# Six blocks of 500, 500, 500, 512, 500 and 500 spectrum columns for two batches, in place of 502 each

## The chip, the core and the metric

The kernel runs on one core of one Trainium2 chip. The core has a matrix engine (PE, with a separate row for its weight loads, PEld), a vector engine (DVE), a scalar engine (ACT), a general engine (POOL) and a queue engine (SP) that issues the DMAs. The metric is the device time of one execution in microseconds (us), lower is better.

## What is computed

```python
X = np.fft.fft(x, axis=1)              # x: 8 batches, 3008 positions, 256 features
X = np.fft.fft(X, axis=2)
x = X.real.astype(np.float32).reshape(8 * 3008, 256)
h = x @ w_in                           # 256 -> 2048
r = np.maximum(h, 0.0)
g = s * (r * r) + b
return g @ w_out                       # 2048 -> 256
```

The real part of the transform of real data has symmetries, so only 1506 spectrum columns of each batch are formed, and each gives two of the 3008 rows of the result.

## The kernel before

**Stages.** For each batch the kernel loads eight tiles of x (`load`), transforms them with matrix tables (`transform`, one call for each half `ph` of the columns), and splits the result into a high and a low part, `spec_h` and `spec_l` (`store`, ACT for the high and POOL for the low part). The 1506 columns are cut into three blocks of `NT = 502`. Each block goes through 16 steps of an MLP, one for each 128 of the 2048 hidden features: 8 batches, 3 blocks and 16 steps make 384 steps.

**One step.** `first_layer` runs six matmuls of 502 columns on PE (two kinds, and three products for each: high by high, high weights by low data, low weights by high data) into PSUM. DVE adds a rank-one term from `ebc`, the broadcast Nyquist row of this block, and forms two rows of hidden values in `h` (L830 to L832). ACT squares them and rounds them to the high part `gh` (L845 to L847), POOL or DVE forms the low part `gl` (L851). `second_layer` runs twelve matmuls of 502 columns (L868): two rows `pm`, two output halves `dh`, and three products. So a step has 18 streams through PE, each behind a weight load of its own of 128 by 128. In the steps of the very first block the streams of row `pm = 0` are 504 columns wide: two more columns of ones give sums of the weights.

**Memory.** A tile that PE streams is `[P, 2, HALF]` with `HALF = 512`: two rows of 2048 bytes in each partition. The 502 columns, of 4 bytes each, start at a row's first byte and end at byte 2008; 504 columns end at byte 2016. They are of the type fp32r, which goes through PE once. The feature fold of the weights and the transforms (L370, L656) run on plain fp32.

**Order.** What each engine does in which order is written out by hand, as a string of letters for the first batch (`START`) and one for each later batch (`BATCH`). `_in_order` fixes the order of each engine's instructions, so nothing is reordered while the kernel runs. The transform of batch n+1 lies among the steps of batch n. `finish` adds scale and bias after a block's last step (L887) and writes it out with two DMAs on SP (L891); `load_e` fetches the next block's `ebc` on SP (L962).

Of the kernel before, what the change touches and what calls it, by code (L numbers as in the profile page):

```python
# [9 lines left out]
F32 = mybir.dt.float32  # L10
# [25 lines left out]
SPLIT = 754  # L36

# [62 lines left out]
def _columns():  # L100

    ks, turned = [], []
    for ph in range(2):
        m = _quarters(ph)
        n = H if ph else Q
        both = np.stack([m, n - m], axis=1)
        sg = np.stack([_SIGMA, -_SIGMA])[None, :, :, None] + 0 * both
        k = both * (1 if ph else 2)
        k, sg = k.reshape(4, 8, G), sg.reshape(4, 8, G)
        if ph == 0:  # L110
            parts = [
                (0, lambda v: v.reshape(2, 4 * G)[:, :-1]), (1, lambda v: v.reshape(4, 2 * G)[:, :-1]),
                (2, lambda v: v), (3, lambda v: v[:, :-1]),
            ]
        else:
            parts = [(0, lambda v: v), (3, lambda v: v), (1, lambda v: v[:, :-1]), (2, lambda v: v[:, :-1])]
# [108 lines left out]


def _in_order(tc):
# [42 lines left out]
def kernel(ctx: ExitStack, tc: tile.TileContext, xq, xn, dft, turn, feat, w_in, w_out, s, b, out):  # L270
# [176 lines left out]
    def nyquist(ph, t, room):  # L447
# [62 lines left out]
                stop=i == len(work) - 1,  # L510
            )
        yield
        e = room if ph else outp.tile([P, 2 * NT], F32, name="e", tag="o")
        to = 0
        for r in range(4):
            at, groups, size, kept = PLACES[ph][r]
# [14 lines left out]

    def block_of(su, blk):
        if (su, blk) not in spec_tiles:
            spec_tiles[su, blk] = [spec_part(part) for part in "hl"]
# [86 lines left out]
    def store(su, ph, parts, low_engine=nc.gpsimd):  # L621

        pieces = []
        for r, o in parts:
            at, groups, size, kept = PLACES[ph][r]
            n = groups * kept
            first = at // NT
            if (at + n - 1) // NT == first:
                pieces.append((
                    first, at - first * NT, n, lambda v, g=groups: v.rearrange("p k (a g) -> p k a g", a=g),  # L630
                    o.rearrange("p k (a g) -> p k a g", a=groups)[:, :, :, :kept],
                ))
            else:
                cut = (first + 1) * NT - at
                pieces.append((first, NT - cut, cut, lambda v: v, o[:, :, :cut]))
                pieces.append((first + 1, 0, n - cut, lambda v: v, o[:, :, cut:]))
# [182 lines left out]

    def first_layer(su, blk, j, ebc):  # L820
        mh, ml = block_of(su, blk)
        held, ps = two_banks()
        ps = ps[:, :, :NT]
        fj = slice(j * P, (j + 1) * P)
        for kind in range(2):
            for i, (w, m) in enumerate(((wd_h, mh), (wd_h, ml), (wd_l, mh))):
                nc.tensor.matmul(ps[:, kind], w[:, kind, fj], m[:, kind], start=i == 0, stop=i == 2)  # L827
        yield
        h = act.tile([P, 2, NT], F32, name="h")
# [4 lines left out]
        step = (su * NBLK + blk) * NJ + j  # L834
        rows = (slice(1, 2), slice(0, 1)) if step in HALVED else (slice(0, 2),)
        gh, gl = halves_of("gh"), halves_of("gl")
        if (su, blk) == (0, 0):

            nc.gpsimd.memset(gh[:, 0, NT:NT + 2].bitcast(F32), 1.0)
            nc.gpsimd.memset(gl[:, 0, NT:NT + 2].bitcast(F32), 0.0)  # L840
        for pm in rows:
            if step in SQUARES_OF_STEPS_ON_VECTOR:
                nc.vector.scalar_tensor_tensor(h[:, pm], h[:, pm], 0.0, h[:, pm], op0=ALU.max, op1=ALU.mult)
            else:
                nc.scalar.activation(h[:, pm], h[:, pm], AF.Relu)  # L845
                nc.scalar.activation(h[:, pm], h[:, pm], AF.Square)  # L846
            nc.scalar.copy(gh[:, pm, :NT], h[:, pm])  # L847
        yield gh, gl
        engine = nc.vector if step in LOWS_OF_STEPS_ON_VECTOR else nc.gpsimd
        for pm in rows:  # L850
            engine.tensor_sub(gl[:, pm, :NT], h[:, pm], gh[:, pm, :NT].bitcast(F32))  # L851
        yield

    def second_layer(po, j, g, sums, end, order):
        gh, gl = g
        start, stop = j == 0, j == NJ - 1
        for pm in order:
            n = NT + 2 if sums and pm == 0 else NT
            work = [
                (dh, l, r, first, last)  # L860
                for l, r, first, last in ((wo_h, gh, True, False), (wo_l, gh, False, False), (wo_h, gl, False, True))
# [9 lines left out]
                )  # L871

    def finish(su, blk, po):
        if (su, blk) == (0, 0):
            for dh in range(2):
                nc.vector.tensor_scalar(bias[:, dh:dh + 1], po[dh][:, NT:NT + 1], sb_b, None, ALU.mult)
        last = (su, blk) == (NB - 1, NBLK - 1)
        for pm in range(2):
            o = outp.tile([P, 2, NT], F32, name="o")
            for dh in range(2):  # L880
                args = sb_s, bias[:, dh:dh + 1]

                dst, src = o[:, dh], po[2 * pm + dh][:, :NT]
# [17 lines left out]
    lo = [spec_part("l") for _ in range(2)]  # L901
    room = read.tile([P, 1024], F32, name="room", tag="spec_h")
    hi = [spec_part("h") for _ in range(2)]
# [49 lines left out]
    step = 0  # L953

    def load_e(n):
        su, blk = divmod(n, NBLK)
        ebc[n] = small.tile([P, NT], F32, name="ebc")
        for ph in range(2):
            first, last = max(0, blk * NT - SPLIT * ph), min((blk + 1) * NT - SPLIT * ph, e_dram[ph].shape[1])
            if first < last:  # L960
                at = first + SPLIT * ph - blk * NT
                nc.sync.dma_start(ebc[n][:, at:at + last - first], e_dram[ph][su, first:last].partition_broadcast(P))  # L962

    def first():
        nonlocal step
        su, blk, j = step // (NBLK * NJ), step // NJ % NBLK, step % NJ
        step += 1
        n = su * NBLK + blk
        if j == NJ // 2 + (NJ // 4 if n == 0 else 0) and n + 1 < NB * NBLK:
# [9 lines left out]
    def second():  # L979
        nonlocal po  # L980
        (su, blk, j), g = pending.pop(0)
        if j == 0:
            po = [ps_o.tile([P, 512], F32, name="po") for _ in range(4)]
        second_layer(
            po, j, g, (su, blk) == (0, 0), (su, blk, j) == (NB - 1, NBLK - 1, NJ - 1),
            (1, 0) if (su * NBLK + blk) * NJ + j in HALVED else (0, 1),
        )
        if j == NJ - 1:
            finish(su, blk, po)
# [24 lines left out]
            next(work[what])  # L1014

    su = 1
    while step < NB * NBLK * NJ:
        work = {}
        if su < NB - 1:
            work = {"l": load(su + 1), "v": transform(su + 1, 0), "o": transform(su + 1, 1)}  # L1020
        for what in BATCH.split():
            if what == "L" and step < NB * NBLK * NJ:
                first()
                go_on_first()
                next(lows.pop(0))
# [40 lines left out]
```

## Time and profile before

| | |
|---|---|
| time, median of 3 runs | 1664.88 us (1663.75 to 1666.82) |
| the profiled execution's own time | 1666.82 us |
| its span | 1663.8 us |
| busy: PE, DVE, ACT, POOL | 1647.9, 1291.8, 1241.5, 908.7 us |
| HBM traffic | 40 GB/s over the span |

The span is what the profiler sees from the first to the last instruction; 3.0 us of the execution lie around it. Busy time is a sum over the whole span. PE's rows are pipelined, so a PE that is busy all the time need not be at its peak: its pace is read from where its matmuls start.

### The profile page before, as it was taken

The page shows a single profiled execution, that of the slowest core. Times are in us where ns is not written, and L with a number is a line of the kernel's source. Part 1 is how long each engine was busy: PE and PEld are TensorE (multiplying, and loading weights), DVE is VectorE, ACT ScalarE, POOL GpSimd, SP SyncE. Part 2 cuts the span into 40 slices and gives each one's busy share as a digit, 9 for nine tenths or more (in the row PEclk, how much of TensorE's full clock was granted, in tenths as well). Part 3 has the DMA queues.
Part 4 walks back from the last instruction along what each step waited for, and adds up shares of the span by engine and source line. Part 5 has one row for each costly group of instructions (what it writes and reads, how often), then busy time and mean ns, then how long its engine had stood idle before and what let it go on. Part 6 is the DMA issues. An engine that isn't in the chain of part 4 may idle for free.

```text
span 1663.8 us, 21402 instructions
## 1 busy us (share of the span) xinstructions
PE 1647.9 (99%) x7592; PEld 1375.8 (83%) x7592; DVE 1291.8 (78%) x2010; ACT 1241.5 (75%) x1300; POOL 908.7 (55%) x538
## 2 busy tenths in 40 slices
PE   9999999999999999999999999999999999999998
PEld 5788888888888888888888888888888888888887
DVE  7999989997779767798677976889767887776453
ACT  4986666677687777877777777777778777687776
POOL 5663334555565555655656556555555555565554
PEclk9999999999999999999999999999999999999999
DMA  8211201120012100120000200112101110000000
GB/s 235 77 39 51 69 20 32 39 70 31 1 32 73 36 32 1 41 73 26 32 28 22 80 10 31 32 33 67 39 3 32 39 50 32 1 32 28 4 26 25
DMA packets 25680, 67.44 MB, mean 41 GB/s; under 512 B 4931, under 2 KB 10371, under 8 KB 25574
## 3 DMA queue, kind: packets, MB, share of 16 engines
q1 hardware_dynamic: 25574, 66.09, 12.8%
q8 instruction: 59, 0.97, 0.2%
q14 instruction: 47, 0.39, 0.1%
HBM read 41.35 MB, written 24.73 MB: 40 GB/s over the span
## 4 chain that ended last, share of the span: by engine, by line
PE 92%; DVE 4%; DMA 2%; issue 1%; ACT 0%; POOLq 0%; SPq 0%; DVEq 0%
PE po L868 59%; PE ab L827 30%; PE ab L656 3%; DVE h L830 1%; DVE h L831 1%; DMA raw<-in_w_in 1%; DMA xt<-in_xq 1%; DVE h L832 1%; PE ab L370 0%; DVE cs L566 0%; DVE xt L561 0%; DMA dft_sb<-in_dft 0%; DMA room<-in_xn 0%; DVE xt L563 0%; DVE uv L403 0%
## 5 line engine op out<-in xcount | busy, mean ns | idle before, releaser
L851 POOL TENSOR_TENSOR gl<-h,gh 128x1004 fp32r<-128x1004 f32 (+1 forms) x365 | 801.7, 2197 | 689.8 <-ACT gh L847 485.0
L845 ACT ACTIVATE h<-h 128x1004 f32<-128x1004 f32 (+1 forms) x380 | 395.4, 1041 | 340.9 <-DVE h L832 339.7
L830 DVE SCALAR_TENSOR_TENSOR h<-ebc,wny,ab 128x502 f32<-128x502 f32 x384 | 281.7, 734 | 299.9 <-PE ab L827 294.6
L868 PE MATMUL po<-gh,wo_h 128*128 128x502 f32 (+1 forms) x1536 | 471.9, 388 | 0.0
L868 PE MATMUL po<-gl,wo_h 128*128 128x502 f32 (+1 forms) x1536 | 468.2, 386 | 0.2 <-POOL gl L851 0.2
L868 PE MATMUL po<-gh,wo_l 128*128 128x502 f32 (+1 forms) x1536 | 468.4, 386 | 0.0
L847 ACT CAST gh<-h 128x1004 fp32r<-128x1004 f32 (+1 forms) x385 | 397.6, 1033 | 34.3 <-PE po L868 15.6
L846 ACT ACTIVATE h<-h 128x1004 f32<-128x1004 f32 (+1 forms) x380 | 396.1, 1042 | 12.1
L868 PEld LDWEIGHTS po<-gl,wo_h 128*128 128x128 f32 x1536 | 288.3, 188 | 55.8 <-POOL gl L851 0.7
L868 PEld LDWEIGHTS po<-gh,wo_l 128*128 128x128 f32 x1536 | 288.4, 188 | 55.3
L868 PEld LDWEIGHTS po<-gh,wo_h 128*128 128x128 f32 x1536 | 285.2, 188 | 51.9
L827 PE MATMUL ab<-spec_h,wd_h 128*128 128x502 f32 x768 | 299.5, 390 | 7.8 <-DVE h L832 6.9
L827 PE MATMUL ab<-spec_l,wd_h 128*128 128x502 f32 x768 | 296.2, 386 | 0.2 <-DVE spec_l L642 0.2
L827 PE MATMUL ab<-spec_h,wd_l 128*128 128x502 f32 x768 | 296.1, 386 | 0.0
L832 DVE TENSOR_TENSOR h<-h,ab 128x502 f32<-128x502 f32 x384 | 260.4, 678 | 13.3
L831 DVE TENSOR_TENSOR h<-h,ab 128x502 f32<-128x502 f32 x384 | 260.2, 678 | 13.2
L827 PEld LDWEIGHTS ab<-spec_h,wd_h 128*128 128x128 f32 x768 | 144.2, 188 | 40.0 <-DVE h L832 11.3
L827 PEld LDWEIGHTS ab<-spec_h,wd_l 128*128 128x128 f32 x768 | 144.1, 188 | 27.7
L827 PEld LDWEIGHTS ab<-spec_l,wd_h 128*128 128x128 f32 x768 | 144.2, 188 | 26.8 <-DVE spec_l L642 0.5
L887 DVE TENSOR_SCALAR o<-po,sb_s,bias 128x502 f32<-128x502 f32 x94 | 68.8, 793 | 8.5 <-PE po L868 8.4
L642 POOL TENSOR_TENSOR spec_l<-o,spec_h 128x384 fp32r<-128x384 f32 (+4 forms) x75 | 60.3, 828 | 18.6 <-ACT spec_h L639 18.1
L561 DVE TENSOR_TENSOR xt<-xt 96x512 f32<-96x512 f32 x56 | 65.1, 1163 | 0.0
(125 smaller groups left out, 735.0 us busy)
## 6 DMA issues: line engine op xcount, KB each, us to landing
xt<-in_xq SPq DMA_DIRECT2D x64, 384.0 KB
out<-o SPq DMA_DIRECT2D x46, 502.0 KB
raw<-in_w_in SPq DMA_DIRECT2D x8, 512.0 KB
raw<-in_w_out SPq DMA_DIRECT2D x8, 512.0 KB
ebc<-e_dram SPq DMA_DIRECT2D x16, 251.0 KB
ebc<-e_dram SPq DMA_DIRECT2D x8, 126.0 KB
out<-o SPq DMA_DIRECT2D x4, 251.0 KB
ebc<-e_dram SPq DMA_DIRECT2D x8, 125.0 KB
```

What stands on the lines that cost most here:

```text
L561: add(t[:, 0::2], t[:, 0::2], t[:, 1::2])
L642: low_engine.tensor_sub(lo, src, hi.bitcast(F32))
L827: nc.tensor.matmul(ps[:, kind], w[:, kind, fj], m[:, kind], start=i == 0, stop=i == 2)
L830: nc.vector.scalar_tensor_tensor(h[:, 0], ebc, wny[:, j:j + 1], ps[:, 0], op0=ALU.mult, op1=ALU.add)
L831: sub(h[:, 1], h[:, 0], ps[:, 1])
L832: add(h[:, 0], h[:, 0], ps[:, 1])
L845: nc.scalar.activation(h[:, pm], h[:, pm], AF.Relu)
L846: nc.scalar.activation(h[:, pm], h[:, pm], AF.Square)
L847: nc.scalar.copy(gh[:, pm, :NT], h[:, pm])
L851: engine.tensor_sub(gl[:, pm, :NT], h[:, pm], gh[:, pm, :NT].bitcast(F32))
L868: nc.tensor.matmul(po[2 * pm + dh][:, :n], l[:, j, dh * P:(dh + 1) * P], r[:, pm, :n], start=start and first, stop=stop and last,)
L887: nc.vector.tensor_scalar(dst, src, *args, ALU.mult, ALU.add)
```

## The change

Two consecutive batches share six blocks. The even batch gives three blocks of 500 columns and keeps its last 6 in a small tile `rest`; the odd batch's first block is those 6 behind 506 of its own, 512 in all, and two blocks of 500 follow. The six blocks have 3012 columns together, as before. Tiles that hold 512 columns start at a row's first byte; those of 500 start four elements, 16 bytes, further on and end at byte 2016. The places of the parts in the second half of the columns are reordered. Output and `ebc` of the shared block come from two batches, so some DMAs become two.

```diff
-NT = 502
-NBLK = 3
+NT = NK
+NBLK = 1
+SHORT = 500
+NBLOCKS = 3
+REST = NK - NBLOCKS * SHORT
...
-    ((754, 1, 192, 192), (1138, 8, 24, 23), (1322, 8, 24, 23), (946, 1, 192, 192)),
+    ((938, 1, 192, 192), (754, 8, 24, 23), (1130, 8, 24, 23), (1314, 1, 192, 192)),
...
+def _stretches(su):
+
+    cuts = (0, SHORT, 2 * SHORT, 3 * SHORT) if su % 2 == 0 else (0, SHORT + REST, 2 * SHORT + REST, NK)
+    own = [(blk, cuts[blk], cuts[blk + 1]) for blk in range(NBLOCKS)]
+    return own + ([(None, cuts[-1], NK)] if su % 2 == 0 else [])
+
+
+def _sources(su, blk):
+
+    _, first, last = _stretches(su)[blk]
+    own = [(su, first, last, 0)]
+    return own + ([(su - 1, NK - REST, NK, last)] if su % 2 and blk == 0 else [])
+
+
+def _width(su, blk):
+    return sum(last - first for _, first, last, _ in _sources(su, blk))
...
-    def halves_of(name):
-
-        return read.tile([P, 2, HALF], F32R, name=name)
-
-    def spec_part(part):
-        return halves_of(f"spec_{part}")[:, :, :NT]
-
+    def halves_of(name, width):
+
+        first = 0 if width == HALF else 4
+        return read.tile([P, 2, HALF], F32R, name=name)[:, :, first:]
+
+    def spec_part(part, width):
+        return halves_of(f"spec_{part}", width)[:, :, :width]
+
+    rest = late.tile([P, 2, REST], F32, name="rest")
...
+                elif blk is None:
+                    nc.scalar.copy(rest, o[:, :, a - at:z - at])
+                else:
+                    pieces.append((blk, a - first, z - a, lambda v: v, o[:, :, a - at:z - at]))
+                if su % 2 and z == SHORT + REST:
+                    pieces.append((blk, z, REST, lambda v: v, rest))
...
-        ps = ps[:, :, :NT]
+        width = _width(su, blk)
+        ps = ps[:, :, :width]
...
-                if last:
-                    nc.sync.dma_start(out[su, blk, :, 2 * pm + dh], o[:, dh])
-            if not last:
-                nc.sync.dma_start(out[su, blk, :, 2 * pm:2 * pm + 2], o)
+                if not last and dh == 0:
+                    continue
+                which = slice(dh, dh + 1) if last else slice(0, 2)
+                for of, a, z, at in _sources(su, blk):
+                    nc.sync.dma_start(
+                        out[of, 0, :, 2 * pm + which.start:2 * pm + which.stop, a:z], o[:, which, at:at + z - a]
+                    )
```

On PE, where the third block of batch 0 gives way to the first of batch 1 (`ab` and `po` are PSUM tiles, `wd` and `wo` the weights of the two layers), the rows before are these:

```order
L868 MATMUL po<-gh,wo_l 128x502 x2
L868 MATMUL po<-gl,wo_h 128x502 x2
L827 MATMUL ab<-spec_h,wd_h 128x502
L827 MATMUL ab<-spec_l,wd_h 128x502
L827 MATMUL ab<-spec_h,wd_l 128x502
```

At the same place of the changed kernel:

```order
L897 MATMUL po<-gh,wo_l 128x500 x2
L897 MATMUL po<-gl,wo_h 128x500 x2
L856 MATMUL ab<-spec_h,wd_h 128x512
L856 MATMUL ab<-spec_l,wd_h 128x512
L856 MATMUL ab<-spec_h,wd_l 128x512
```

No matmul has moved, and PE has as many rows as before; only the widths differ, here 500 and then 512 where 502 stood. The 504 of the first block become 502.

On SP, during the first blocks of batch 1 (`xt` are tiles of x for a later batch, the two `e_dram` tensors hold the two halves of the Nyquist row), the rows before are these:

```order
L962 DMA ebc<-e_dram_109 128x502
L552 DMA xt<-in_xq 96x1024 x2
L891 DMA out<-o 128x1004 x2
L962 DMA ebc<-e_dram_109 128x252
L962 DMA ebc<-e_dram_110 128x250
L552 DMA xt<-in_xq 96x1024 x5
L891 DMA out<-o 128x1004 x2
```

And in the changed kernel:

```order
L995 DMA ebc<-e_dram_109 128x506
L995 DMA ebc<-e_dram_110 128x6
L575 DMA xt<-in_xq 96x1024 x2
L922 DMA out<-o 128x2x500 x2
L995 DMA ebc<-e_dram_109 128x248
L995 DMA ebc<-e_dram_110 128x252
L575 DMA xt<-in_xq 96x1024 x5
L922 DMA out<-o 128x2x506
L922 DMA out<-o 128x2x6
L922 DMA out<-o 128x2x506
L922 DMA out<-o 128x2x6
```

The order is the same; an issue for 6 columns stands behind each one that serves the shared block.

## Rows read from the trace of the kernel before

**Rows 1.** The page: busy time and share of each engine; the chain that ended last.

```profile
PE 1647.9 (99%) x7592; PEld 1375.8 (83%) x7592; DVE 1291.8 (78%) x2010; ACT 1241.5 (75%) x1300; POOL 908.7 (55%) x538
...
PE 92%; DVE 4%; DMA 2%; issue 1%; ACT 0%; POOLq 0%; SPq 0%; DVEq 0%
PE po L868 59%; PE ab L827 30%; PE ab L656 3%; DVE h L830 1%; DVE h L831 1%; DMA raw<-in_w_in 1%; DMA xt<-in_xq 1%; DVE h L832 1%; PE ab L370 0%; DVE cs L566 0%; DVE xt L561 0%; DMA dft_sb<-in_dft 0%; DMA room<-in_xn 0%; DVE xt L563 0%; DVE uv L403 0%
```

**Rows 2.** Windows of one batch each: length, engines' busy us, PE clock, DMA.

```profile
486.00:686.00 200.00, 200.00 (x928) 169.03 (x927) 155.00 (x244) 151.59 (x154) 113.25 (x58) 1.00 0.11 36
686.00:886.00 200.00, 200.00 (x928) 169.02 (x927) 155.28 (x245) 151.57 (x155) 113.19 (x58) 1.00 0.11 36
886.00:1086.00 200.00, 200.00 (x928) 169.02 (x927) 155.53 (x244) 151.55 (x155) 113.26 (x58) 1.00 0.11 36
1286.00:1486.00 200.00, 200.00 (x928) 169.07 (x927) 155.58 (x244) 151.55 (x155) 112.93 (x59) 1.00 0.10 32
```

**Rows 3.** Waits of PE's weight loads, 486 to 1486 us: total, times, longest.

```profile
PEld ab L827 <- DVE h L832: 0.4, 1, 0.4
```

**Rows 4.** The chain from 1560 us: start, duration, engine, count of instructions.

```profile
1560.16 5.36 PE po L868 x24
1565.52 2.68 PE ab L827 x12
```

**Rows 5.** Groups by form: the matmuls that carry the MLP (count | busy, mean ns).

```profile
L868 PE MATMUL po<-gh,wo_h 128*128 128x502 f32 x1504 | 461.9, 388 | 0.0
L827 PE MATMUL ab<-spec_h,wd_h 128*128 128x502 f32 x768 | 299.5, 390 | 7.8 <-DVE h L832 6.9 <-DVE wd_l L297 0.8
L868 PE MATMUL po<-gh,wo_h 128*128 128x504 f32 x32 | 10.0, 393 | 0.0
```

**Rows 6.** Timeline of PE, a step of the first block: start, duration.

```profile
114.22 0.62 PE L868 MATMUL po<-gh,wo_h 128*128 128x504 f32 x2
114.67 0.62 PE L868 MATMUL po<-gh,wo_l 128*128 128x504 f32 x2
115.13 0.61 PE L868 MATMUL po<-gl,wo_h 128*128 128x504 f32 x2
115.58 0.62 PE L868 MATMUL po<-gh,wo_h 128*128 128x502 f32 x2
```

**Rows 7.** Timeline of PE: plain fp32 matmuls of 512 columns, and the next.

```profile
90.43 1.45 PE L370 MATMUL ab<-cs,feat_sb 128*128 128x512 f32 x3
91.72 1.03 PE L656 MATMUL ab<-dft_sb,lf 96*128 96x96 f32 x8
```

**Rows 8.** Timeline of PE: twelve L868 matmuls of one step (502 columns), and the next.

```profile
250.79 0.63 PE L868 MATMUL po<-gh,wo_h 128*128 128x502 f32 x2
...
253.59 1.03 PE L656 MATMUL ab<-dft_sb,cs 96*128 96x96 f32 x8
```

**Rows 9.** Groups by form: the smallest pieces of a block's high and low part.

```profile
L642 POOL TENSOR_TENSOR spec_l<-o,spec_h 128x116 fp32r<-128x116 f32 x8 | 4.0, 498 | 0.0
...
L639 ACT CAST spec_h<-o 128x116 fp32r<-128x116 f32 x8 | 2.3, 284 | 0.0
```

**Rows 10.** Timeline of SP, block ends of one batch: DMA issues.

```profile
800.54 1.78 SPq L891 DMA_DIRECT2D out<-o  x2
802.37 0.44 SPq L962 DMA_DIRECT2D ebc<-e_dram  x1
868.55 1.75 SPq L891 DMA_DIRECT2D out<-o  x2
870.40 1.14 SPq L962 DMA_DIRECT2D ebc<-e_dram  x2
```

More of the change, by code (lines that the diff above doesn't have):

```diff
@@ L115, in _columns @@
         else:
-            parts = [(0, lambda v: v), (3, lambda v: v), (1, lambda v: v[:, :-1]), (2, lambda v: v[:, :-1])]
+            parts = [(1, lambda v: v[:, :-1]), (0, lambda v: v), (2, lambda v: v[:, :-1]), (3, lambda v: v)]
         for r, cut in parts:
@@ L512, in nyquist @@
         yield
-        e = room if ph else outp.tile([P, 2 * NT], F32, name="e", tag="o")
+        e = room if ph else outp.tile([P, 2 * HALF], F32, name="e", tag="o")
         to = 0
@@ L533, in block_of @@
         if (su, blk) not in spec_tiles:
-            spec_tiles[su, blk] = [spec_part(part) for part in "hl"]
+            spec_tiles[su, blk] = [spec_part(part, _width(su, blk)) for part in "hl"]
         return spec_tiles[su, blk]
-    def halves_of(name):
-        return read.tile([P, 2, HALF], F32R, name=name)
-    def spec_part(part):
-        return halves_of(f"spec_{part}")[:, :, :NT]
+    def halves_of(name, width):
[4 more added lines that the diff above has]
+    rest = late.tile([P, 2, REST], F32, name="rest")
     folded = {}
@@ L626, in store @@
             n = groups * kept
[L627 to L636, printed above, removed]
+            for blk, first, last in _stretches(su):
+                a, z = max(at, first), min(at + n, last)
+                if a >= z:
+                    continue
+                if z - a == n:
+                    pieces.append((
+                        blk, at - first, n, lambda v, g=groups: v.rearrange("p k (a g) -> p k a g", a=g),
+                        o.rearrange("p k (a g) -> p k a g", a=groups)[:, :, :, :kept],
+                    ))
+                elif blk is None:
[4 more added lines that the diff above has]
+                    pieces.append((blk, z, REST, lambda v: v, rest))
         views = [[f(t[:, :, at:at + n]) for t in block_of(su, blk)] for blk, at, n, f, _ in pieces]
@@ L828, in first_layer @@
         yield
-        h = act.tile([P, 2, NT], F32, name="h")
+        h = act.tile([P, 2, width], F32, name="h")
         nc.vector.scalar_tensor_tensor(h[:, 0], ebc, wny[:, j:j + 1], ps[:, 0], op0=ALU.mult, op1=ALU.add)
@@ L833, in first_layer @@
         banks.give(held)
-        step = (su * NBLK + blk) * NJ + j
+        step = (su * NBLOCKS + blk) * NJ + j
         rows = (slice(1, 2), slice(0, 1)) if step in HALVED else (slice(0, 2),)
-        gh, gl = halves_of("gh"), halves_of("gl")
+        gh, gl = halves_of("gh", width), halves_of("gl", width)
         if (su, blk) == (0, 0):
-            nc.gpsimd.memset(gh[:, 0, NT:NT + 2].bitcast(F32), 1.0)
-            nc.gpsimd.memset(gl[:, 0, NT:NT + 2].bitcast(F32), 0.0)
+            nc.gpsimd.memset(gh[:, 0, width:width + 2].bitcast(F32), 1.0)
+            nc.gpsimd.memset(gl[:, 0, width:width + 2].bitcast(F32), 0.0)
         for pm in rows:
@@ L846, in first_layer @@
                 nc.scalar.activation(h[:, pm], h[:, pm], AF.Square)
-            nc.scalar.copy(gh[:, pm, :NT], h[:, pm])
+            nc.scalar.copy(gh[:, pm, :width], h[:, pm])
         yield gh, gl
@@ L850, in first_layer, with second_layer @@
         for pm in rows:
-            engine.tensor_sub(gl[:, pm, :NT], h[:, pm], gh[:, pm, :NT].bitcast(F32))
+            engine.tensor_sub(gl[:, pm, :width], h[:, pm], gh[:, pm, :width].bitcast(F32))
         yield
-    def second_layer(po, j, g, sums, end, order):
+    def second_layer(po, j, g, width, sums, end, order):
         gh, gl = g
@@ L857, in second_layer @@
         for pm in order:
-            n = NT + 2 if sums and pm == 0 else NT
+            n = width + 2 if sums and pm == 0 else width
             work = [
@@ L873, in finish @@
     def finish(su, blk, po):
+        width = _width(su, blk)
         if (su, blk) == (0, 0):
             for dh in range(2):
-                nc.vector.tensor_scalar(bias[:, dh:dh + 1], po[dh][:, NT:NT + 1], sb_b, None, ALU.mult)
-        last = (su, blk) == (NB - 1, NBLK - 1)
+                nc.vector.tensor_scalar(bias[:, dh:dh + 1], po[dh][:, width:width + 1], sb_b, None, ALU.mult)
+        last = (su, blk) == (NB - 1, NBLOCKS - 1)
         for pm in range(2):
-            o = outp.tile([P, 2, NT], F32, name="o")
+            o = outp.tile([P, 2, width], F32, name="o")
             for dh in range(2):
                 args = sb_s, bias[:, dh:dh + 1]
-                dst, src = o[:, dh], po[2 * pm + dh][:, :NT]
+                dst, src = o[:, dh], po[2 * pm + dh][:, :width]
                 if last and dh:
@@ L887, in finish @@
                     nc.vector.tensor_scalar(dst, src, *args, ALU.mult, ALU.add)
-                if last:
-                    nc.sync.dma_start(out[su, blk, :, 2 * pm + dh], o[:, dh])
-            if not last:
-                nc.sync.dma_start(out[su, blk, :, 2 * pm:2 * pm + 2], o)
+                if not last and dh == 0:
+                    continue
+                which = slice(dh, dh + 1) if last else slice(0, 2)
[3 more added lines that the diff above has]
+                    )
     tiles = {}
@@ L900 @@
     minus = unit[:R, 2 * R:6 * R].rearrange("p (i l) -> p i l", i=4)
-    lo = [spec_part("l") for _ in range(2)]
+    lo = [spec_part("l", SHORT) for _ in range(2)]
     room = read.tile([P, 1024], F32, name="room", tag="spec_h")
-    hi = [spec_part("h") for _ in range(2)]
+    hi = [spec_part("h", SHORT) for _ in range(2)]
     for k in range(2):
@@ L955, in load_e @@
     def load_e(n):
[L956 to L962, printed above, removed]
+        su, blk = divmod(n, NBLOCKS)
+        ebc[n] = small.tile([P, _width(su, blk)], F32, name="ebc")
+        for of, a, z, at in _sources(su, blk):
+            for ph, (first, last) in enumerate(((0, SPLIT), (SPLIT, NK))):
+                lo, hi = max(a, first), min(z, last)
+                if lo < hi:
+                    nc.sync.dma_start(
+                        ebc[n][:, at + lo - a:at + hi - a],
+                        e_dram[ph][of, lo - first:hi - first].partition_broadcast(P),
+                    )
     def first():
         nonlocal step
-        su, blk, j = step // (NBLK * NJ), step // NJ % NBLK, step % NJ
+        su, blk, j = step // (NBLOCKS * NJ), step // NJ % NBLOCKS, step % NJ
         step += 1
-        n = su * NBLK + blk
-        if j == NJ // 2 + (NJ // 4 if n == 0 else 0) and n + 1 < NB * NBLK:
+        n = su * NBLOCKS + blk
+        if j == NJ // 2 + (NJ // 4 if n == 0 else 0) and n + 1 < NB * NBLOCKS:
             load_e(n + 1)
@@ L984, in second @@
         second_layer(
-            po, j, g, (su, blk) == (0, 0), (su, blk, j) == (NB - 1, NBLK - 1, NJ - 1),
-            (1, 0) if (su * NBLK + blk) * NJ + j in HALVED else (0, 1),
+            po, j, g, _width(su, blk), (su, blk) == (0, 0), (su, blk, j) == (NB - 1, NBLOCKS - 1, NJ - 1),
+            (1, 0) if (su * NBLOCKS + blk) * NJ + j in HALVED else (0, 1),
         )
@@ L1016 @@
     su = 1
-    while step < NB * NBLK * NJ:
+    while step < NB * NBLOCKS * NJ:
         work = {}
@@ L1021 @@
         for what in BATCH.split():
-            if what == "L" and step < NB * NBLK * NJ:
+            if what == "L" and step < NB * NBLOCKS * NJ:
                 first()
```

## The prediction

> **What bounds the kernel now.** I read the page first. PE is busy for 99% of the span, and the chain that ended last runs through PE for 92% of it, nearly all in the two MLP lines [rows 1]. That alone does not say that PE could not go faster, so I went on to the windows, one batch each: from 486 us on PE is busy for 200.00 of 200 us, DVE for some 155, ACT for 152, POOL for 113, and the granted clock is 1.00, the level of 2.4 GHz [rows 2]. The waits say whether PE hangs on somebody: over five batches its weight loads waited once, for 0.4 us [rows 3]. So in the steady part nothing holds PE but PE. The time is the number of matmuls times the distance from one start to the next, and that distance is what the change can move.
>
> **The pace of a stream.** The chain gives starts: 24 matmuls of 502 columns take 5.36 us and 12 take 2.68 us [rows 4], 223.3 ns each. At 2.4 GHz a column is 0.417 ns, so 502 columns are 209.2 ns, and each matmul carries 14.2 ns in which no column goes through. The mean durations of 388 or 390 ns [rows 5] overlap each other and are no pace. Two other widths stand in the trace. Six streams of 504 columns run from 114.22 to 115.58 us [rows 6], 226.7 ns each: two columns more, worth 0.8 ns of clock, cost 3.4 ns. Plain fp32 matmuls of 512 columns run three in 1.29 us [rows 7], 430 ns each, which is twice 215.0: those data go through twice, at half the bytes for each cycle, and carry only 1.7 ns over the clock for each pass of 213.3. And the same 502 columns, with the same instructions, once ran twelve in 2.80 us [rows 8], 233.3 ns each. So a stream's extra time isn't a constant: it depends on the width by more than the clock explains, and can settle at more than one level.
>
> **What the change moves.** A step has 18 matmuls and there are 384 steps: 6912 streams, 1543.5 us at 223.3 ns, 93% of the span. The counts agree (1504 and 32 for one of three products of the second layer, 768 for one of the first) [rows 5]. After the change 5/6 of them, 5760, have 500 columns and start 16 bytes further on, and 1152 have 512 columns from a row's first byte. The columns in total stay the same, 3012 for each pair of batches, so at a fixed extra for each matmul nothing would change.
>
> *A stream of 500 from byte 16.* No row shows this start. From below: the lowest extra that any long stream shows is that of the plain fp32 rows, so 215.0 less 12 columns of 0.417, 210.0 ns. From above: 226.7 ns, what 504 columns take that end at the same byte 2016; the worst level that a row shows is 233.3 less 0.8. I take what the two fp32r widths give when the line through them is carried two columns down: 223.3 - 3.4 = 219.9 ns. They are the nearest rows, of the same type and at the same rate; for the start I put nothing. That is 5760 x 3.4 ns = 19.6 us less.
>
> *A stream of 512.* From below 215.0 ns, the plain fp32 rows for one pass; from above 226.7 + 8 x 0.417 = 230.0, the 504 with its extra kept. The line through 502 and 504 would give 240.3 ns, but it can't hold for long, since it would ask for an extra of 27 ns, more than even the slow level's 24.1. The fp32 rows have the width and the filled row of 2048 bytes, the 504 rows have the type and the rate; I take the middle, 222.5. That is 1152 x 0.8 = 0.9 us less.
>
> *The rest.* ACT gets 8 instructions more, the copies into `rest` and out of it, of 12 elements; POOL 4. The nearest rows, of 116 elements, take 284 ns on ACT and 498 on POOL [rows 9], from above; below lies nothing. That is at most 2.3 and 2.0 us in all, on engines that are idle for 48 and 87 us in each batch [rows 2]. Without that cover they would be worth as much on the path. The larger block makes a step's instructions on DVE, ACT and POOL 2% longer, the shorter ones 0.4% shorter; over a pair of batches that is nothing. SP issues 16 DMAs more. An issue of `out` takes 0.89 us and of `ebc` 0.44 to 0.57 [rows 10], so at most 14 us over the whole run, on a queue that stands still between blocks; behind it wait only tiles of x for a later batch and the next block's `ebc`, due half a block later. I put all of this at 0.
>
> *Whether the others keep up.* A batch now takes 200 us. DVE, the fullest, needs 155.6 [rows 2]; 20 us less over eight batches asks for 197.5, and the whole extra removed for some 189. DVE would then be at 82%. With one wait of 0.4 us in five batches [rows 3] I see no queue that is near its limit, so PE's gain would come through whole.
>
> **The sum.** 19.6 + 0.9 = 20.5 us less. The profiled execution took 1666.82 us, so 1646.3 by its own account; it is the slowest of the three, 1.9 us above the median of 1664.88. Taken to the median: **1644.4 us**, 1.2% faster.
>
> **The rivals.**
>
> *The extra of the 500s goes for the most part.* If it comes from how a row's end meets the next row's start, a width of whole 16-byte pieces and a later start may remove it. For this speak the plain fp32 rows, which show that PE can chain long matmuls with 1.7 ns between them [rows 7], and that the extra reacts so sharply to two columns [rows 4, 6]. Against it: 504 is also a whole number of 16-byte pieces, and it is worse than 502. At the lower bounds: 5760 x 13.3 + 1152 x 8.3 = 76.6 + 9.6 = 86.2 us less, 1578.7 us; with 500 at half way, 216.7, and 512 as now, 38 us less, 1626.9 us.
>
> *Nothing changes.* If each matmul carries a fixed extra and a column only its clock, five streams of 222.5 and one of 227.5 are six of 223.3, and the time stays at 1664.9. For it speaks that the columns are the same in number; against it the 504 rows, which broke that rule by 2.6 ns [rows 6]. The Trainium skill has this rule (TensorE: Matmul & The Clock Gate, Back-to-back issue gap): in a warm stream a matmul follows the last one after its columns at 2.4 GHz and a constant of 2.5 ns. By it 502 columns would take 211.7 ns, and the trace disagrees with that by 11.6 ns; the plain fp32 rows agree with it, pass by pass, within 1 ns. As the page has a constant that doesn't depend on width or start, by the page this change is worth nothing.
>
> *The end counts, and it gets slower.* A stream of 500 from byte 16 ends at byte 2016, just as the 504 do. If the extra hangs on where a row ends, or if the later start is paid as four empty columns, the 500s take what the 504s take: 226.7 ns, 5760 x 3.4 = 19.6 us more, and the 512, at 230.0, 1152 x 6.7 = 7.7 us more: 1692.2 us. It decides from the point at which a 500 costs more than 223.5 ns, with the 512s at their middle. That one width ran at 233.3 as well [rows 8] shows that a worse level is within reach.
>
> **How the numbers follow.** My forecast (500 at about 220 ns, 1632 to 1661 us) has a chance of 0.38, the larger removal (below 1632 us) 0.30, no change within 0.2% 0.11, slower 0.21. 0.2% is about what a measurement of this kernel can tell from no change. So faster 0.68, same 0.11, slower 0.21. For 8 in 10 the range reaches down to 1598 us, which leaves out the deepest third of the second case, 0.1, and up to 1690, which leaves out a good third of the slower one, 0.08.
>
> **What would show it.** In the profile after, the distance between starts decides everything: 24 streams of 500 should take 5.28 us in the chain where 502 took 5.36, and 12 streams of 512 some 2.67. If the 500s stand at 5.05 to 5.2 us, the second case is right; at 5.34 with the 512s at 2.73, the third; at 5.44, the fourth. A window of one batch should still show PE busy throughout, and DVE, ACT and POOL with the same busy time as now; new waits of PE for DVE or POOL in the list of waits would say that the others did not keep up. What would make the forecast wrong is above all the start at byte 16, which no row of the trace has, and a pace that settles at another level.

## The result and the profile after

| | before | after |
|---|---|---|
| time, median | 1665.43 us (4 runs, 1663.75 to 1666.82) | 1678.74 us (4 runs, 1678.45 to 1679.25) |
| span of the profiled execution | 1663.8 us | 1677.3 us |

The ratio is 1.0081 with a 95% interval of 1.0063 to 1.0098: the change makes the kernel 13.3 us slower. The prediction was 1644.4 us, a gain. Among the experiments below one execution, of the kernel before with cheap rows, was a slow one of 5497.44 us; it stands in that version's median of 1660.15 us, which is 1659.83 us without it.

The page of the changed kernel first, busy time and then the chain that ended last, where [rows 1] show the kernel before:

```profile
PE 1645.9 (98%) x7592; PEld 1374.0 (82%) x7592; DVE 1334.0 (80%) x2010; ACT 1242.9 (74%) x1308; POOL 975.6 (58%) x542
...
PE 79%; DVE 14%; issue 3%; DMA 2%; ACT 1%; POOL 0%; POOLq 0%; SPq 0%; DVEq 0%; ACTq 0%
```

PE is busy for 2 us less, but POOL for 67 us more and DVE for 42 us more, with 4 instructions more on POOL and none on DVE. DVE's share of the chain has gone from 4% to 14%. The windows of about one batch, to be held against [rows 2]:

```profile
489.00:691.00 202.00, 199.29 (x928) 168.31 (x926) 163.17 (x244) 151.55 (x157) 121.64 (x59) 1.00 0.12 35
691.00:894.00 203.00, 200.57 (x931) 168.87 (x930) 164.36 (x245) 152.10 (x155) 121.91 (x58) 1.00 0.12 35
```

PE is no longer busy throughout: it stands idle for more than 2 us in each window. DVE has grown by 8 us a batch and POOL by 8; ACT and the clock are as they were. The chain shows the pace of PE's streams, first of 500 columns (600 us on) and then of 512 (1103 us on), as in [rows 4] for 502:

```profile
601.44 2.64 PE po L897 x12
604.08 1.32 PE ab L856 x6
605.40 2.64 PE po L897 x12
...
1107.63 2.72 PE ab L856 x12
1110.35 5.44 PE po L897 x24
```

Twelve streams of 500 take 2.64 us, 220.0 ns each; 24 of 512 take 5.44 us, 226.7 ns each. So the 500s run here at the pace that was forecast, to 0.1 ns, and most of the loss lies elsewhere. I put together all distances between neighbouring starts of MLP matmuls. Those under 240 ns average 223.5 ns before (6729 of them, all of 502 columns), and after 220.6 for the 500s (5531) and 227.9 for the 512s (1126); over all 500s and 512s that is 5663 x 2.9 - 1152 x 4.4 = 11 us gained. The longer distances are pauses. What they hold beyond the median distance of their width was 16.6 us in total before and is 41.0 us after: 24.4 us lost. The two make 13 us, and the span is 13.5 us longer.

The list of waits says who caused the pauses (total us, times, longest). PE, its weight loads, and DVE:

```profile
PE ab L856 <- DVE h L861: 21.0, 22, 1.8
...
PEld ab L856 <- DVE h L861: 34.9, 39, 2.3
...
DVE h L859 <- POOL gl L880: 96.8, 51, 3.9
```

The same three in the kernel before:

```profile
PE ab L827 <- DVE h L832: 6.9, 7, 1.4
...
PEld ab L827 <- DVE h L832: 11.3, 12, 1.8
...
DVE h L830 <- POOL gl L851: 2.2, 2, 1.9
```

So PE waits for DVE, and DVE's first instruction of a step waits for POOL more often than before. Whether these two waits belong together is taken up with the four buffers below. The groups name the work that grew: POOL's low part, and two DVE groups (count | busy, mean ns | idle before and its cause):

```profile
L880 POOL TENSOR_TENSOR gl<-h,gh 128x1000 fp32r<-128x1000 f32 x302 | 715.6, 2370 | 536.8 <-ACT gh L876 442.2 <-DVE h L860 16.5 <-PE ab L856 15.3
L880 POOL TENSOR_TENSOR gl<-h,gh 128x1024 fp32r<-128x1024 f32 x61 | 149.5, 2451 | 98.8 <-ACT gh L876 70.9 <-DVE h L860 16.0 <-PE po L897 5.6
...
L584 DVE TENSOR_TENSOR xt<-xt 96x512 f32<-96x512 f32 x56 | 73.7, 1315 | 0.0
L588 DVE TENSOR_TENSOR cs<-xt 96x256 f32<-96x256 f32 x56 | 61.7, 1101 | 0.7
```

And the same groups before:

```profile
L851 POOL TENSOR_TENSOR gl<-h,gh 128x1004 fp32r<-128x1004 f32 x363 | 799.2, 2202 | 688.5 <-ACT gh L847 483.7 <-DVE h L831 141.1 <-DVE h L830 27.3
L561 DVE TENSOR_TENSOR xt<-xt 96x512 f32<-96x512 f32 x56 | 65.1, 1163 | 0.0
L565 DVE TENSOR_TENSOR cs<-xt 96x256 f32<-96x256 f32 x56 | 39.2, 700 | 0.7
```

POOL's low part has four elements fewer in each partition and takes 168 ns longer, 8%; with 2% more elements it takes 249 ns longer. The two DVE groups belong to the transform and are untouched by the change, yet they take 152 and 401 ns longer. One stretch of the changed kernel's timeline shows how the two hang together (start, duration, idle time before and its cause):

```profile
916.00 2.36 POOL L880 TENSOR_TENSOR gl<-h,gh 128x1000 fp32r<-128x1000 f32 x1 [0.70 <-ACT gh L876]
916.10 2.80 DVE L584 TENSOR_TENSOR xt<-xt 96x512 f32<-96x512 f32 x1
...
919.59 2.34 POOL L880 TENSOR_TENSOR gl<-h,gh 128x1000 fp32r<-128x1000 f32 x1 [1.23 <-ACT gh L876]
...
919.73 2.48 DVE L588 TENSOR_TENSOR cs<-xt 96x256 f32<-96x256 f32 x1
...
922.14 0.41 DVE L589 TENSOR_TENSOR cs<-xt 96x256 f32<-96x256 f32 x1
...
922.48 0.72 DVE L859 SCALAR_TENSOR_TENSOR h<-ebc,wny,ab 128x500 f32<-128x500 f32 x1
...
924.53 0.68 DVE L584 TENSOR_TENSOR xt<-xt 96x512 f32<-96x512 f32 x1
924.66 0.19 PEld L856 LDWEIGHTS ab<-spec_h,wd_h 128*128 128x128 f32 x1 [0.59 <-DVE h L861]
```

An `xt` of 512 elements takes 0.68 us when POOL is quiet (the row at 924.53). The one at 916.10 begins 0.1 us after a low part on POOL, and ends 0.54 us after it, 2.80 us in all. The `cs` at 919.73 does the same, 2.48 us where the next one of the same form, at 922.14, takes 0.41. DVE stands still behind POOL. Then L859 comes late, with it the release of PSUM after L861, and the weight load of PE's next first layer waits 0.59 us. The step's own instructions on DVE (L859 to L861), which take one input from PSUM, are not stretched: they took 800.6 us in all, against 802.3 before. The Trainium skill states the reason (SBUF — State Buffer, Who interferes with whom): a VectorE instruction with two inputs in SBUF and a GpSimd instruction that reads SBUF share a port, and whoever comes second is blocked for the whole of the other's instruction; these rows agree, with 2.80 us behind 2.36.

What the diff did to POOL is a matter of addresses. In the built programs before and after, `h`, `gh` and `gl` begin at multiples of 64 bytes (in the versions below with a wider `h` at multiples of 32). The rows of `h` (its `pm` = 0 and 1) lie as close as their width lets them, those of `gh` and `gl` 2048 bytes apart. Before, `h` row 1 began at byte 2008 and `gh` row 1 at 2048: 40 apart, not a multiple of 16; row 0 of both began at 0. After, `h` has rows at 0 and 2000 and `gh` at 16 and 2064, distances 16 and 64; in the blocks of 512 both have 0 and 2048. So my theory: a row is dear on POOL when its two inputs lie a multiple of 16 bytes apart, and before the change one row in two escaped by luck.

### The profile page after: what moved, and what is told of

Same layout as the page of the kernel before. It is cut to its first block, busy times and chain, and to the rows that moved or that the text cites. A ratio compares the mean times of both kernels' runs of the same rounds, so it can differ in the third digit from the quotient of the medians.

```text
span 1677.3 us, 21438 instructions
## 1 busy us (share of the span) xinstructions
PE 1645.9 (98%) x7592; PEld 1374.0 (82%) x7592; DVE 1334.0 (80%) x2010; ACT 1242.9 (74%) x1308; POOL 975.6 (58%) x542
## 4 chain that ended last, share of the span: by engine, by line
PE 79%; DVE 14%; issue 3%; DMA 2%; ACT 1%; POOL 0%; POOLq 0%; SPq 0%; DVEq 0%; ACTq 0%
PE po L897 50%; PE ab L856 25%; PE ab L684 3%; DVE h L859 3%; DVE h L860 3%; DVE xt L584 2%; DVE h L861 2%; DVE xt L586 1%; DVE cs L589 1%; DVE cs L588 1%; DMA raw<-in_w_in 1%; DMA xt<-in_xq 1%; DVE xt L585 0%; ACT h L875 0%; ACT h L874 0%
## 5 line engine op out<-in xcount | busy, mean ns | idle before, releaser
L880 POOL TENSOR_TENSOR gl<-h,gh 128x1000 fp32r<-128x1000 f32 (+2 forms) x365 | 867.9, 2378 | 636.7 <-ACT gh L876 514.2
L874 ACT ACTIVATE h<-h 128x1000 f32<-128x1000 f32 (+2 forms) x380 | 395.3, 1040 | 351.2 <-DVE h L861 347.6
L859 DVE SCALAR_TENSOR_TENSOR h<-ebc,wny,ab 128x500 f32<-128x500 f32 (+1 forms) x384 | 280.8, 731 | 269.5 <-PE ab L856 150.5
L897 PE MATMUL po<-gh,wo_h 128*128 128x500 f32 (+2 forms) x1536 | 470.2, 387 | 0.0
L897 PE MATMUL po<-gl,wo_h 128*128 128x500 f32 (+2 forms) x1536 | 466.6, 385 | 0.8 <-POOL gl L880 0.8
L897 PE MATMUL po<-gh,wo_l 128*128 128x500 f32 (+2 forms) x1536 | 466.2, 385 | 0.0
L876 ACT CAST gh<-h 128x1000 fp32r<-128x1000 f32 (+2 forms) x385 | 397.4, 1032 | 35.2 <-PE po L897 15.8
L875 ACT ACTIVATE h<-h 128x1000 f32<-128x1000 f32 (+2 forms) x380 | 396.2, 1043 | 12.1
L856 PE MATMUL ab<-spec_h,wd_h 128*128 128x500 f32 (+1 forms) x768 | 301.5, 393 | 21.9 <-DVE h L861 21.0
L856 PE MATMUL ab<-spec_l,wd_h 128*128 128x500 f32 (+1 forms) x768 | 295.5, 385 | 0.2 <-DVE spec_l L670 0.2
L856 PE MATMUL ab<-spec_h,wd_l 128*128 128x500 f32 (+1 forms) x768 | 295.3, 385 | 0.0
L860 DVE TENSOR_TENSOR h<-h,ab 128x500 f32<-128x500 f32 (+1 forms) x384 | 260.0, 677 | 13.2
L861 DVE TENSOR_TENSOR h<-h,ab 128x500 f32<-128x500 f32 (+1 forms) x384 | 259.9, 677 | 13.2
L856 PEld LDWEIGHTS ab<-spec_h,wd_l 128*128 128x128 f32 x768 | 144.3, 188 | 26.6
L856 PEld LDWEIGHTS ab<-spec_l,wd_h 128*128 128x128 f32 x768 | 144.4, 188 | 24.4 <-DVE spec_l L670 0.5
```

Of the source, the lines that this page charges most:

```text
L876: nc.scalar.copy(gh[:, pm, :width], h[:, pm])
L880: engine.tensor_sub(gl[:, pm, :width], h[:, pm], gh[:, pm, :width].bitcast(F32))
L897: nc.tensor.matmul(po[2 * pm + dh][:, :n], l[:, j, dh * P:(dh + 1) * P], r[:, pm, :n], start=start and first, stop=stop and last,)
```

## Experiments

Runs of one group share the runs of the kernel before: its median was 1664.89 us for the first four, 1665.63 for those with the cheap kernel before, with 8 and 4 bytes moved and with four buffers, 1666.95 for the one with `gl` moved, 1665.03 for the last two; a ratio is to that. Where only one execution was made there is no ratio.

**Dear rows alone.** The kernel before, with `h` rows moved to 2048 bytes apart and nothing else.

```diff
-h = act.tile([P, 2, NT], F32, name="h")
+h = act.tile([P, 2, HALF], F32, name="h")[:, :, :NT]
```

> The kernel before, with the two rows of h 2048 bytes apart instead of 2008, so that both rows of h stand at the same place within 16 bytes as the rows of gh. Theory P (POOL's low part costs 0.17 us more for each row of h and gh whose distance is a multiple of 16 bytes, DVE is held up behind it, and PE waits for DVE): gl takes 2.36 us on POOL instead of 2.19, the streams stay at 223.3 ns, PE's waits grow by some 20 us, about 1687 us. Rival S (the start at byte 16 makes POOL slow): gl stays at 2.19 us, 1665 us. Rival W (a faster PE finds DVE not ready, whatever POOL takes): the pace is the old one, so 1665 us.

1686.14 us, ratio 1.0127 (1.0111 to 1.0142): 21 us slower, with every stream as before (223.7 ns mean under 240 ns). Its low part and two of its waits:

```profile
L851 POOL TENSOR_TENSOR gl<-h,gh 128x1004 fp32r<-128x1004 f32 x363 | 869.0, 2394 | 640.2 <-ACT gh L847 517.6 <-DVE h L831 69.9 <-PE po L868 20.7
...
DVE h L830 <- POOL gl L851: 81.9, 42, 3.8
...
PE ab L827 <- DVE h L832: 20.5, 19, 1.8
```

One slice in one line brings all the signs of the changed kernel. The loss needs neither the new widths nor the new start.

**Cheap rows in the changed kernel.** `h` 8 bytes further on, its rows 2064 bytes apart: both rows now lie 8 bytes from `gh`'s.

```diff
-h = act.tile([P, 2, width], F32, name="h")
+h = act.tile([P, 2, HALF + 4], F32, name="h")[:, :, 2:2 + width]
```

> The changed kernel with h moved by 8 bytes and its rows 2064 bytes apart, so that no row of h has the place of gh's row within 16 bytes; the streams are left as they are. Theory P: gl at about 2.01 us, less than in the kernel before, since now both rows are free; waits of PE back to what they were, streams at 220.0 and 226.7 ns, about 1650 us. Rival S: gl stays at 2.36 us and the time at 1679 us. Rival W: gl may fall, but the waits of PE for DVE stay, about 1675 to 1679 us.

1648.11 us, ratio 0.9899 (0.9884 to 0.9914). It beats the kernel before by 1.0% and the changed one by 30.6 us. Its page, low part and PE's wait:

```profile
PE 1634.3 (99%) x7592; PEld 1376.9 (84%) x7592; DVE 1263.7 (77%) x2010; ACT 1243.2 (76%) x1308; POOL 830.0 (50%) x542
...
L880 POOL TENSOR_TENSOR gl<-h,gh 128x1000 fp32r<-128x1000 f32 x302 | 597.7, 1979 | 630.4 <-ACT gh L876 508.7 <-DVE h L859 37.4 <-DVE h L860 36.8
...
PE ab L856 <- DVE h L861: 1.6, 2, 1.1
```

POOL falls to 1979 ns, lower than in the kernel before, and DVE's total falls with it by 70 us.

**Cheap rows, 500s from byte 0.** The same with `first = 0`, so that only the width of the streams differs from the kernel before, not their start.

```diff
-first = 0 if width == HALF else 4
+first = 0
```

> As the run with h moved by 8 bytes, but with the blocks of 500 streamed from a row's first byte. If the width alone sets the pace (500 columns: 33 times 6.67 ns), the streams take 220.0 ns and the time is that run's, about 1650 us. If the start at byte 16 is what brings 220, the 500s take 223 to 227 ns and the time is 17 to 38 us longer.

1670.12 us, ratio 1.0034 (1.0022 to 1.0045). The chain, from 623 us:

```profile
623.64 2.68 PE ab L856 x12
626.32 5.36 PE po L897 x24
```

Here 500 columns run at 223.3 ns, in the steps around 610 us at 226.7 (12 in 2.72 us); their mean under 240 ns is 225.2. With 500 columns alone nothing is gained: it is the start at byte 16 that brings 220.0.

**502 columns from byte 16.** The kernel before with all its streams 16 bytes further on.

```diff
-return read.tile([P, 2, HALF], F32R, name=name)
+return read.tile([P, 2, HALF], F32R, name=name)[:, :, 4:]
```

> The kernel before with all streams 16 bytes further on (502 columns from byte 16, 504 in the first block). If the start doesn't matter for PE, 223.3 ns for each stream; if four bytes times four of empty columns are paid, about 226.7 to 233. Theory P: gl on POOL as in the kernel before, 2.19 us, since one row of h still differs by 8 bytes; 1665 us at the old pace. Rival S: gl 2.36 us or more and new waits of PE, 1680 us or more.

1694.47 us, ratio 1.0178 (1.0163 to 1.0193). Twelve streams take 2.75 us in the chain, and the mean distance under 240 ns is 228.9 ns; the low part stays at 2185 ns on average, against 2202 before. So the start at byte 16 is not what makes POOL slow (one of my rivals), and of the two widths it helps the 500 and harms the 502.

**Cheap rows in the kernel before.**

```diff
-h = act.tile([P, 2, NT], F32, name="h")
+h = act.tile([P, 2, HALF + 4], F32, name="h")[:, :, 2:2 + NT]
```

> The kernel before with h moved by 8 bytes and its rows 2064 bytes apart: the streams keep 502 columns and 223.3 ns, and only POOL's low part gets cheaper. Theory P: gl at about 1.97 us, DVE held up less, and only the few waits of PE that the kernel before has (some 10 us) shrink: about 1659 us. If most of what the changed kernel gains with h moved came from POOL and not from the streams, this one would come near 1648 us; if POOL's time didn't matter here, 1665 us.

1660.15 us, ratio 0.9967 (0.9954 to 0.998); PE's wait for `h` falls from 6.9 to 1.5 us.

```profile
L851 POOL TENSOR_TENSOR gl<-h,gh 128x1004 fp32r<-128x1004 f32 x363 | 720.5, 1985 | 758.9 <-ACT gh L847 538.0 <-DVE h L831 131.9 <-DVE xt L561 27.9
```

So of the 17 us by which the best version beats the kernel before, some 5 are POOL's and 12 those of the rest of the change, the streams above all.

**Is it the place of `h`, or its place against `gh`?** The version above with `gh`, `gl` and the spectrum moved 8 bytes as well.

```diff
-return read.tile([P, 2, HALF], F32R, name=name)
+return read.tile([P, 2, HALF], F32R, name=name)[:, :, 2:]
```

> The kernel before with h and all streamed tiles moved by 8 bytes, so that h and gh stand at the same place within 16 bytes again, both off a multiple of 16. If the distance of the two inputs sets POOL's price: gl at 2.38 us. If it is h's own place off a multiple of 16 bytes: gl at 1.97 us. The pace of 502 columns from byte 8 is not known: 223 to 229 ns.

One execution: 1685.35 us, PE waits 18.8 us.

```profile
L851 POOL TENSOR_TENSOR gl<-h,gh 128x1004 fp32r<-128x1004 f32 x363 | 867.3, 2389 | 640.5 <-ACT gh L847 477.5 <-DVE h L831 111.8 <-PE po L868 27.7
```

With `h` where it was cheap, but the two inputs again 0 and 16 bytes apart, the low part is dear: the distance counts. The streams, now from byte 8, kept an average of 223.7 ns, so the 20 us are not theirs.

**Are 4 bytes enough?** The changed kernel with `h` 4 bytes further on.

```diff
-h = act.tile([P, 2, width], F32, name="h")
+h = act.tile([P, 2, HALF + 4], F32, name="h")[:, :, 1:1 + width]
```

> The changed kernel with h moved by 4 bytes, rows 2064 bytes apart. If any distance that is no multiple of 16 bytes will do, gl takes 1.97 us and the time is about 1648 us; if a multiple of 8 is asked for, gl lies between that and 2.36 us.

One execution: 1678.12 us.

```profile
L880 POOL TENSOR_TENSOR gl<-h,gh 128x1000 fp32r<-128x1000 f32 x302 | 714.5, 2366 | 537.3 <-ACT gh L876 441.6 <-PE po L897 14.3 <-DVE h L860 14.0
```

No: rows 4 bytes apart (modulo 16) are as dear as rows at 0, so the theory's "multiple of 16" was too narrow.

**Input or output?** `gl` begins where `gh` begins, so all this could as well be the distance of `h` from the output. The version with dear rows, and `gl` alone 8 bytes further on:

```diff
-gh, gl = halves_of("gh"), halves_of("gl")
+gh, gl = halves_of("gh"), halves_of("gl")[:, :, 2:]
```

> The kernel before with the rows of h 2048 bytes apart, so that both lie a multiple of 16 bytes from gh, and with gl 8 bytes further on, so that both lie 8 bytes (modulo 16) from the output gl. Theory that the place of the two inputs, h and gh, decides POOL's price: 2.37 to 2.39 us for each low part as in the runs with dear rows, PE waits for DVE some 20 us, time near 1686 us. Theory that the place of h against the output gl decides: 1.98 us, PE waits under 2 us, time near 1660 us. In between (about 2.19 us): both count. A third of the second layer's streams then start at byte 8, where 502 columns took 223.4 ns on the whole; that should move nothing.

One execution: 1684.47 us.

```profile
L851 POOL TENSOR_TENSOR gl<-h,gh 128x1004 fp32r<-128x1004 f32 x363 | 865.4, 2384 | 641.7 <-ACT gh L847 485.1 <-DVE h L831 123.9 <-PE ab L827 9.5
```

The two inputs decide, not the output. The time is near what was expected for another reason than the one expected: PE waited for DVE only 3.5 us, but its streams ran at 226.8 ns on average, those of the spectrum at byte 0 among them. Why they slowed down I did not find out.

**Does PE wait because `h` comes free late?** DVE's wait for POOL (96.8 us) says that L859 needs a buffer of `h` that POOL still reads. The changed kernel with four buffers instead of three from the fourth block on:

```diff
-h = act.tile([P, 2, width], F32, name="h")
+step = (su * NBLOCKS + blk) * NJ + j
+if step < 48:
+    h = act.tile([P, 2, width], F32, name="h")
+else:
+    h = wst.tile([P, 2, width], F32, name="h", tag="raw")
```

> The changed kernel with four buffers for h instead of three from the second batch on, at the same places within 64 bytes, so POOL's low part stays at 2.36 us. If PE waits because h comes free late (DVE's first instruction of a step waits for POOL's low part of three steps before), the 97 us of those DVE waits go, and the time falls towards 1650 us. If PE waits because DVE's instructions stand still while POOL works on the same ports, the time stays at 1672 to 1679 us, and DVE's instructions on xt and cs stay as long as they are.

1677.07 us, ratio 1.0065 (1.0049 to 1.008): no real help. Its DVE and POOL rows:

```profile
L584 DVE TENSOR_TENSOR xt<-xt 96x512 f32<-96x512 f32 x56 | 73.2, 1306 | 0.0
...
DVE h L863 <- POOL gl L884: 60.1, 27, 3.8
...
PE ab L856 <- DVE h L865: 20.9, 20, 1.8
```

The wait for a buffer falls by 37 us and PE's wait not at all; DVE's `xt` is held as long as ever. So PE's wait does not hang on that part of it. As 60.1 us of buffer waits remain, the run alone does not exclude the rest, but the trace of the changed kernel does: in the 15 us before each of the 39 waits of PE's weight loads, L859 never once waited for POOL. In 35 of these 39 stretches DVE's instructions with both inputs in SBUF took, in sum, at least 2.1 us more than the shortest of their form. So L859 waits for a buffer in other places, and what is left for PE's waits is DVE standing still behind POOL, as the timeline showed; no run takes that away and leaves POOL dear.

**Do waits and pace add up?** From the third batch on, a batch took 202.5 us on average after the change and 203.7 in the version with dear rows alone, though PE's paces differ. That looked like a floor under a batch. The changed kernel with `first = 0`, as above, but with dear rows:

> The changed kernel with the blocks of 500 starting at byte 0, as in the run from byte 0 before, but with h where the change has it, so POOL's low part stays at its dear price (2.35 to 2.39 us). Theory that the dear price sets a floor under a batch: with it a batch took 202.7 us on the mean in the changed kernel and 203.6 us in the kernel before with dear rows, though PE's pace differed. Then PE's slower streams (225.2 ns in place of 220.6 for the 500s) cost nothing here: batches of 202 to 204 us, 1677 to 1682 us. Theory that waits and pace add up: the dear price cost 30.6 us between the changed kernel and the one with h moved 8 bytes; on top of the 1670.1 us of the cheap one from byte 0 that gives 1700 us.

1696.74 us, ratio 1.019 (1.0175 to 1.0205). There is no floor: with slower streams a batch took 205.2 us, and PE still waited for DVE.

```profile
L880 POOL TENSOR_TENSOR gl<-h,gh 128x1000 fp32r<-128x1000 f32 x302 | 716.9, 2374 | 550.7 <-ACT gh L876 396.7 <-DVE h L860 93.1 <-DVE h L859 14.2
...
PE ab L856 <- DVE h L861: 18.4, 18, 1.6
```

Dear rows cost 1696.74 - 1670.12 = 26.6 us here, 30.6 at the faster pace, and 1686.14 - 1660.15, some 26, in the kernel before. In these three pairs they add to whatever PE's pace gives. The run with `gl` moved is an exception: at 226.8 ns its pauses, summed as in the first section, were 13.4 us with dear rows, fewer than the 16.6 of the kernel before; why is open.

**One dear row of two in the changed kernel.** The rows of `h` 2056 bytes apart, which gives POOL the price it had before.

```diff
-h = act.tile([P, 2, width], F32, name="h")
+h = act.tile([P, 2, HALF + 2], F32, name="h")[:, :, :width]
```

> The changed kernel with the rows of h 2056 bytes apart, so that one of its two rows lies a multiple of 16 bytes from gh's and the other doesn't: POOL's low part should cost what it cost before, 2.18 us. Waits in proportion to the price: halfway between the changed kernel (2.37 us, 1678.7) and the one with h moved 8 bytes (1.98 us, 1648.1), near 1663 us. Floor: DVE's busy time falls by half of 70 us, 4.4 us a batch, which takes the floor from 202.7 to some 198.5 us, below PE's own 198.8: near 1650 us, with PE waits for DVE of a few us.

1657.72 us, ratio 0.9953 (0.9936 to 0.997).

```profile
L880 POOL TENSOR_TENSOR gl<-h,gh 128x1000 fp32r<-128x1000 f32 x302 | 658.2, 2180 | 578.1 <-ACT gh L876 480.7 <-DVE h L860 23.4 <-DVE xt L584 21.7
...
PE ab L856 <- DVE h L861: 8.7, 9, 1.4
```

The price is 2180 ns, as expected. The time lies between the two expectations. In the changed kernel the first 0.20 us on each low part cost 9.6 us, the next 0.19 us another 21. This is the change with POOL's price as it was: 7.3 us faster than the kernel before, where 20.5 had been forecast.

## Why the prediction was wrong

**The bound.** That PE bounds the kernel and that nothing holds it between 486 and 1486 us was right for the kernel before. The 6.9 us of waits that it had lay mostly earlier: moving `h` alone shortened the first two batches from 205.4 and 206.7 us to 202.5 and 202.1, and left the later ones at 200.3. I had looked where there was nothing to see.

**The 500s.** The pace was right, 219.9 ns forecast and 220.0 in the chain (220.6 on average), but by luck: I carried the line through 502 and 504 two columns down and put nothing for the start. 500 columns from byte 0 take 223.3 to 226.7 ns, 502 from byte 16 take 228.9. The start did it, together with the width. There are also 5664 such streams, not 5760, as 96 of the first block are 502 wide. On the averages they gained 16 us in place of 19.6.

**The 512s.** The term was mis-sized: 222.5 ns forecast, 226.7 measured, inside the bounds of 215.0 and 230.0. In place of a gain of 0.9 us that is a loss of 1152 x 3.4 = 3.9, and 5 on the averages. The lower bound supposed that plain fp32 data go through twice; no run here shows more than the 430 ns. All streams together gave 11 us by their distances and 12 by the runs (the best version against the kernel before with the same cheap rows), where the sum had 20.5.

**The rest.** Of the work on DVE, ACT and POOL the prediction said that the larger block makes it 2% longer, the shorter ones 0.4% shorter, and that "over a pair of batches that is nothing". This is the step that failed and turned the sign: the price of POOL's low part was taken to go with its width alone, and it went from 2.20 to 2.37 us with fewer elements. With the price as it was the change gains 7.3 us, with the new one it loses 13.3; the term that was put at nothing is worth 1678.74 - 1657.72 = 21.0 us. That the rows of `h` would come to lie elsewhere against those of `gh` follows from the diff. The kernel before had a hint that it matters, the two low parts of a single row at its start:

```profile
48.34 1.08 POOL L851 TENSOR_TENSOR gl<-h,gh 128x502 fp32r<-128x502 f32 x1 [0.58 <-ACT gh L847]
50.16 1.42 POOL L851 TENSOR_TENSOR gl<-h,gh 128x502 fp32r<-128x502 f32 x1 [0.74 <-ACT gh L847]
```

The first is row 1, the second row 0, the same form at two prices; with both rows cheap they took 1.07 and 1.20 us.

**Whether the others keep up.** "I see no queue that is near its limit, so PE's gain would come through whole" failed with it. It rested on DVE's share of 78%. The share says nothing of how long DVE stands still at a bad moment: 8 us more in a batch of 200 gave PE 24 us more of pauses over the run. Even at POOL's old price some of the gain was lost: the one dear row cost 5.5 us in the kernel before (1665.63 - 1660.15) and 9.6 at the faster pace.

**The rivals.** None named POOL. The two that were about faster streams or no change fell with the measured pace. The section of the Trainium skill that the prediction cites for the second (TensorE: Matmul & The Clock Gate, Back-to-back issue gap) gives its constant for an isolated matmul and not for streams behind weight loads, so the rule was carried too far. The third, that it gets slower because a stream's end counts, has the right sign, but its price of 226.7 ns for a 500 was not there; its condition, a 500 dearer than 223.5 ns, was not met. What the prediction gave as a sign against itself, new waits of PE for DVE and a POOL and DVE that are busier, is what came.

**The account.** From the kernel before: 5 us less if its one dear row went, 12 us less from the streams, 30.6 us more from two dear rows at the new pace. That makes 13.6 us more; 13.3 were measured. These are steps along one chain of versions, so they must come out near the whole, and their agreement proves nothing. PE's pauses are a check of their own: summed as in the first section they are 9.5 us in the changed kernel with cheap rows, 19.0 with one dear row and 41.0 with two, steps of 9.5 and 22.0 us where the times rose by 9.6 and 21.0. That two inputs' distance sets POOL's price, and that this price sets the time, is shown by the runs. That PE's waits come about through DVE's being blocked is read from the traces, not isolated by a run.

## What to carry to other kernels

When a change touches the widths or starts of tiles, list for each two-input instruction on POOL how far its inputs lie apart before and after, and measure one of them; here 8 bytes in one tile were worth 30 us of 1679. An engine at 55% can hold up one at 99% if it blocks a third between them, so look at the longest single instructions of the neighbours, not at their shares. And look at the waits of the whole run, the first batches too, before calling an engine's slack free.

## What was not expected of the hardware

POOL's subtraction of two fp32 inputs, 1000 elements in each partition, took 1.98 us with both rows 8 bytes apart (modulo 16), 2.18 with one, and 2.36 to 2.37 with none, whether those lay 0 or 4 bytes apart. Row 1 alone, the first low part of a run, shows it too: 128x502 took 1.08 us in the kernel before and 128x500 1.26 us in the changed one. Distances of 12 (modulo 16) were not tried, and why 8 bytes help stays open. DVE, which makes 20 of the low parts, has no such price: the same subtraction of 1000 elements took 1.19 us there in the median with both rows dear, with one and with none.

The pace of fp32r streams depends on width and first byte together, and not smoothly: 500 from byte 16 220.0 ns, 500 from byte 0 223.3 or 226.7, 502 from byte 0 223.3, 502 from byte 8 223.7 and from byte 16 228.9 (both on average), 504 and 512 from byte 0 226.7. What sets it stays open; the same instructions can run at two paces in different steps of one run.
